# Attention and feed-forward in one kernel: three score steps in any two of three banks, one exponential for both heads in the first pairs, and rests copied by VectorE or GpSimd

## The chip, the cores and the metric

One core of one Trainium2 chip. The engines are TensorE (PE, matmuls; PEld are its weight loads), VectorE (DVE), ScalarE (ACT), GpSimd (POOL) and SyncE (SP, which issues most DMAs). The metric is the time of one execution in microseconds (us) on the device; lower is better. Three runs of the kernel before took 423.41, 424.69 and 424.93 us.

## The reference

Eight batches, 12 heads, 448 rows, 64 columns a head; then a feed-forward over 8 x 448 = 3584 rows of 768 columns and 2048 hidden columns.

```python
def rmsnorm(x, g):
    rms = np.sqrt(np.mean(x * x, axis=-1, keepdims=True) + 1e-06)
    return x / rms * g
q_n, k_n = (rmsnorm(q, g_q), rmsnorm(k, g_k))
scores = scale * np.matmul(q_n, k_n.transpose(0, 1, 3, 2))
attn = softmax(scores)                       # over the last axis
x = np.matmul(attn, v), heads side by side   # [3584, 768]
h = x @ w_in
g = h * np.clip(h + 3.0, 0.0, 6.0) / 6.0
out = g @ w_out
```

(The softmax and the reordering are abbreviated here; the rest is the reference's text.)

## The kernel before, in words

**Pairs.** Two heads are one *pair*; there are 48 pairs, six to a batch. 448 rows are three full tiles of 128 and a *rest* of 64; the rests of the two heads of a pair share one tile. In the first pairs (`PD` = `MB` = 6) Q, K and V are loaded *dense*: a partition holds seven rows of one head, the two heads lie in the two halves of the partitions, and each block of 64x64 is transposed by itself (14 or 16 small transposes a tensor). From pair 6 on they are loaded in the form of 128 partitions by 4 tiles, with a DMA for the main rows and one or two for the rest.

**The steps of a pair.** Squares (`square`, L398, any of GpSimd, ScalarE), their sums (`sums`, VectorE), the inverse root by Ln and Exp (`rstd`, ScalarE), normalizing (`normalize`: L427 dense, L429 else; GpSimd, or VectorE for the pairs of `DN`, here pairs 0 and 1), transposing (`transposes` by TensorE up to pair 11, a transposing DMA from pair 12 on), and the copies `put_q` (scaled by g' = g_q g_k / 8, L465 and L467) and `put_k`. Then four *score steps*: one for the rest tile (i = NT, both heads in one matmul of 128 rows, a bank of 448 columns) and three for the full tiles (two matmuls of 64 rows, one a head, two banks). Each is followed by its exponentials on ScalarE (`expo`, L492; `expo_head`, L497) into `eR` or `eD`, and by `weigh` (L513), eight or five thin matmuls with V that gather the pair's output and its row sums in the bank `av`. `eR` holds the rest's columns twice, so that both heads can be read as 128 columns. When all four are weighed, `divide` (VectorE) makes x, `x_out` (TensorE, later a DMA) transposes it, `put_x` stores it.

**Banks.** PSUM has eight banks: two double ones `sc` (units 0 and 1, for scores), three single ones `ps` (units 2, 3, 4, for the feed-forward and the transposes) and `av`. Up to pair 7 (`PB` = 8) the score steps come one by one, up to pair 23 (`P3` = 24) two full steps together, from pair 24 on three at once: the third takes units 2 and 3 (`THIRD`), so that one bank is left to the feed-forward until their exponentials are done.

**Feed-forward.** `h_mm` (L561) multiplies x with `w_in` in 16 pieces a batch of six matmuls; ScalarE makes `t_sb` (`relu`, L567) and VectorE the gate (`gate`, L572). `y_mm` (L580) multiplies with `w_out`, 16 matmuls for 384 columns; the result is copied out of its bank (`y_copy`, L379, ScalarE or VectorE) and stored. The weights come by GpSimd's DMA queue (`load_w`), `w_in` in five pieces.

**What sets the order.** All instructions are put in order at build time by a planner (`Plan`) that runs a model of the engines. Each operation has a key, the engines that may do it with their costs, and what it depends on. An engine takes the ready operation with the least key; where several engines may do it, the one with the least of time free plus cost times a factor (`PRICE`, and `FIRST` up to 45 us). Feed-forward items come from two lanes, and fill TensorE by a credit (`share`, `DUE`, `FILL`). DMAs are modelled too (`SLOW`, `BEGIN`, `AHEAD`, `LATE`), and the load of a pair is held back by a small memset on GpSimd (`hold`, L796) until the norms of an earlier pair are done. On the chip each engine then goes through its list in this order, and waits at an instruction until its semaphores are there. So any changed cost or factor can move any instruction.

## Time and profile before

| | |
|---|---|
| median of 3 runs | 424.69 us (423.41 to 424.93) |
| the profiled execution's own time | 423.99 us |
| its span | 422.1 us |
| TensorE's granted clock | 1.0 |
| HBM read, written | 45.61 MB, 11.01 MB |

The span runs from the first instruction to the last. Busy time of an engine is the time in which one of its instructions ran; matmuls are pipelined, and a run of them counts as busy throughout. Lines with `<-` name what ended an engine's idle time. A row of a timeline begins with start and length in us; a row of groups ends with busy us, the mean ns of one, and the idle time before them.

### The profile page before, as it was taken

The page shows a single profiled execution, that of the slowest core. Times are in us where ns is not written, and L with a number is a line of the kernel's source. Part 1 is how long each engine was busy: PE and PEld are TensorE (multiplying, and loading weights), DVE is VectorE, ACT ScalarE, POOL GpSimd, SP SyncE. Part 2 cuts the span into 40 slices and gives each one's busy share as a digit, 9 for nine tenths or more (in the row PEclk, how much of TensorE's full clock was granted, in tenths as well). Part 3 has the DMA queues.
Part 4 walks back from the last instruction along what each step waited for, and adds up shares of the span by engine and source line. Part 5 has one row for each costly group of instructions (what it writes and reads, how often), then busy time and mean ns, then how long its engine had stood idle before and what let it go on. Part 6 is the DMA issues. An engine that isn't in the chain of part 4 may idle for free.

```text
span 422.1 us, 9498 instructions
## 1 busy us (share of the span) xinstructions
PE 406.6 (96%) x3692; PEld 237.1 (56%) x3692; DVE 210.6 (50%) x436; ACT 291.7 (69%) x713; POOL 201.3 (48%) x215
## 2 busy tenths in 40 slices
PE   2989999999999999999999999999999999999997
PEld 1565655455555555555555556565556555555565
DVE  7775978455444676457364664546243152042100
ACT  5899986766888988897869977789583243243211
POOL 5998956747676647756575676681000000000000
PEclk9999999999999999999999999999999999999999
DMA  8999899999998959988896968943420301100122
GB/s 253 252 217 235 155 235 176 198 244 176 189 246 208 245 109 201 233 195 202 158 248 168 248 122 198 255 106 77 76 64 13 88 0 39 75 2 37 76 75 76
DMA packets 124561, 65.12 MB, mean 154 GB/s; under 512 B 77412, under 2 KB 121060, under 8 KB 124516
## 3 DMA queue, kind: packets, MB, share of 16 engines
q1 hardware_dynamic: 116144, 57.76, 61.2%
q0 software_dynamic: 8080, 6.29, 10.2%
q8 instruction: 29, 0.48, 0.5%
q10 hardware_dynamic: 292, 0.46, 0.3%
q14 instruction: 16, 0.13, 0.1%
HBM read 45.61 MB, written 11.01 MB: 134 GB/s over the span
## 4 chain that ended last, share of the span: by engine, by line
PE 81%; ACT 5%; DMA 5%; issue 2%; DVE 2%; POOL 2%; SPq 1%; POOLq 0%; DVEq 0%; ACTq 0%
PE ps L580 34%; PE ps L561 29%; PE av L513 9%; PE sc L476 6%; DMA v_st<-in_v_dram 3%; ACT eD L492 3%; DMA qkT<-qkn 2%; PE ps L476 1%; DMA qk_st<-in_q_dram 1%; POOL qkn L429 1%; DVE ssq L406 1%; ACT t_sb L567 1%; PE ps L446 1%; SPq L376 1%; PE sc L561 1%
## 5 line engine op out<-in xcount | busy, mean ns | idle before, releaser
L561 PE MATMUL ps<-xT,w_in_sb 128*128 128x448 bf16 x750 | 165.4, 352 | 1.5 <-ACT eD L497 1.1
L580 PE MATMUL ps<-w_out_sb,gT 128*128 128x384 bf16 (+1 forms) x896 | 162.5, 323 | 0.0
L572 DVE SCALAR_TENSOR_TENSOR gT<-t_sb,ps 128x448 bf16<-128x448 f32 x125 | 76.9, 620 | 110.5 <-ACT t_sb L567 109.6
L492 ACT ACTIVATE eD<-sc 128x768 bf16<-128x768 f32 x240 | 113.3, 567 | 6.0 <-PE sc L476 5.6
L580 PEld LDWEIGHTS <-gT 128*128 128x128 bf16 x912 | 83.8, 98 | 57.2 <-issue 8.8
L561 PEld LDWEIGHTS <-w_in_sb 128*128 128x128 bf16 x768 | 69.8, 98 | 57.6 <-issue 6.1
L429 POOL TENSOR_TENSOR qkn<-qk_st,rstd 128x512 bf16<-128x512 f32 x84 | 85.2, 1043 | 25.0 <-ACT rstd L419 24.7
L403 POOL TENSOR_TENSOR sq<-qk_st 128x1024 f32<-128x1024 f32 (+2 forms) x50 | 81.6, 1642 | 31.8 <-DMA qk_st<-in_q_dram 18.5
L567 ACT ACTIVATE t_sb<-ps 128x448 f32<-128x448 f32 x125 | 69.8, 562 | 31.1 <-PE ps L561 28.5
L513 PEld LDWEIGHTS <-eD 128*128 128x128 bf16 x1152 | 52.4, 98 | 23.2 <-issue 6.3
L406 DVE TENSOR_REDUCE ssq<-sq 128x16 f32<-128x1024 f32 (+2 forms) x50 | 57.7, 1156 | 8.9 <-POOL sq L403 5.9
L379 ACT COPY y_sb<-ps 128x384 f32<-128x384 f32 (+1 forms) x43 | 20.6, 478 | 57.4 <-PE ps L580 57.3
L513 PE MATMUL av<-vaug,eD 128*128 128x65 bf16 x1152 | 58.9, 194 | 0.0
L476 PE MATMUL sc<-qkT 64*128 64x448 bf16 (+1 forms) x288 | 52.8, 358 | 3.2 <-DVE qkT L467 1.1
L379 POOL CAST vaug<-v_st 128x512 bf16<-128x512 f32 x29 | 17.7, 620 | 39.2 <-PE av L513 38.7
L497 ACT ACTIVATE eD<-ps 128x448 bf16<-128x448 f32 (+2 forms) x72 | 25.1, 419 | 15.7 <-PE ps L476 15.7
L492 ACT ACTIVATE eR<-sc 128x448 bf16<-128x448 f32 x96 | 32.9, 412 | 3.1 <-PE sc L476 2.9
L523 DVE RECIPROCAL rden<-av 128x7 f32<-128x7 f32 x48 | 9.7, 202 | 40.4 <-PE av L513 40.2
L476 PEld LDWEIGHTS <-qkT 64*128 64x128 bf16 (+1 forms) x336 | 15.4, 95 | 22.2 <-issue 14.5
L465 ACT ACTIVATE qkT<-qkT,gprime 128x448 bf16<-128x448 bf16 x36 | 24.8, 691 | 1.7 <-DMA qkT<-qkn 1.7
L529 DVE TENSOR_TENSOR xn<-av,rden 128x384 bf16<-128x384 f32 x42 | 23.4, 557 | 1.5
L513 PEld LDWEIGHTS <-eR 128*128 128x128 bf16 x240 | 16.7, 99 | 7.2 <-issue 1.9
(72 smaller groups left out, 177.8 us busy)
## 6 DMA issues: line engine op xcount, KB each, us to landing
qk_st<-in_k_dram SPq DMA_DIRECT2D x21, 384.0 KB, 4.0
qk_st<-in_q_dram SPq DMA_DIRECT2D x21, 384.0 KB, 5.5
v_st<-in_v_dram SPq DMA_DIRECT2D x21, 384.0 KB, 5.9
out_dram<-y_sb SPq DMA_DIRECT2D x20, 384.0 KB, 2.4
w_out_sb<-in_moe_w_out_dram POOLq DMA_DIRECT2D x4, 768.0 KB, 11.1
out_dram<-y_sb SPq DMA_DIRECT2D x15, 192.0 KB, 2.7
w_in_sb<-in_moe_w_in_dram POOLq DMA_DIRECT2D x3, 768.0 KB, 9.5
v_st<-in_v_dram SPq DMA_DIRECT2D x22, 64.0 KB, 5.7
```

The source lines that it names most:

```text
L379: (eng.copy if eng is nc.scalar else eng.tensor_copy)(out=out, in_=in_)
L403: eng.tensor_tensor(out=sq, in0=x, in1=x, op=A_MULT)
L406: nc.vector.tensor_reduce(out=packed(p, ssq_r[:, p % NR, a]), in_=packed(p, sq_r[m % 2][:, a]), axis=mybir.AxisListType.X, op=A_ADD,)
L429: eng.tensor_tensor(out=qkn_r[p % NQ][:, a].rearrange("p t h d -> p h t d"), in0=qk_st[:, a, p % NS], in1=by[:, a].rearrange("p (h t) -> p ...
L476: nc.tensor.matmul(out=(bank(u[h]) if isinstance(u, tuple) else bank(u, h))[:, 0:S], lhsT=qkT[rows, 0, i * P:(i + 1) * P], rhs=qkT[rows, 1 ...
L492: nc.scalar.activation(out=out, in_=in_, func=EXP, bias=0.0, scale=1.0)
L497: nc.scalar.activation(out=e[:, c:c + cols.stop - cols.start], in_=src[:, cols], func=EXP, bias=0.0, scale=1.0)
L513: nc.tensor.matmul(out=av_ps[:, c:c + n], lhsT=e_part(p, i, h, j), rhs=va[:, i].rearrange("p h d -> p (h d)")[:, h * W:h * W + n], start=f ...
L561: nc.tensor.matmul(out=bank(m)[:, 0:S], lhsT=w_in_sb[:, kt, f * P:(f + 1) * P], rhs=xT[:, kt, b % NX, x_slot(b)], start=(kt == 0), stop=(k ...
L567: nc.scalar.activation(out=t[:], in_=bank(m)[:, 0:S], func=RELU, bias=0.5, scale=1.0 / 6.0,)
L572: nc.vector.scalar_tensor_tensor(out=gT[:, f, (b % 2) * S:(b % 2 + 1) * S], in0=t[:], scalar=1.0, in1=bank(m)[:, 0:S], op0=A_MIN, op1=A_MULT,)
L580: nc.tensor.matmul(out=bank(m)[:, 0:n], lhsT=gT[:, f, c0:c0 + P], rhs=w_out_sb[:, f, c:c + n], start=(f == 0), stop=(f == NFT - 1),)
```

## The change

It has these parts.

1. **Three at once.** `THIRD` is now a list of (2, 3), (3, 4), (2, 4), and the planner takes whichever two are free. `P3` goes from 24 to 32, `PB` from 8 to 4. While a burst is due, feed-forward may take banks 3, 2 and 4, not 4 alone.
2. **One early exponential.** In the first six pairs (`TURNED` = 6) the second head's score is made in two matmuls, rest columns first, so that the two heads of a full step lie in one even pattern and one exponential of 896 columns does both. Before there were two: 768 main columns, 128 rest columns.
3. **Rests repeated.** The second copy of `eR`'s rest columns is no longer a second exponential of 64 columns but a copy within `eR` by GpSimd or VectorE (`repeat`), and `weigh` of a rest waits for it.
4. **K and V dense only in pairs 0 and 1** (`PK` = 2); Q stays dense up to pair 5. K and V of pairs 2 to 5 come in the other form; K of these pairs is loaded in the other form, with rest loads and cleared rests of its own, transposed in four pieces instead of 16, and squared with a padded eighth block.
5. **Start.** VectorE normalizes only K of pair 0; the rest goes to GpSimd. Q of pair 1 comes by SP, not by ScalarE's queue. g' is mixed by GpSimd. `w_in` comes in six pieces (256, 256, 256, 256, 512, 512).
6. **The planner's figures**: prices, due times, DMA model, keys, and holds.

What the two built programs hold, by engine (only what differs and matters):

| engine, operation | before | after |
|---|---|---|
| PE transposes 64x64 of Q, K | 168 (+12 of zeros) | 112 (+4) |
| PE transposes 128x128 of Q, K | 48 | 64 |
| PE scores cut into 384 and 64 columns | 0 | 18 |
| ACT exponentials of 64 rest columns into eR | 48 | 0 |
| ACT exponentials 768 and 128 columns | 120 and 120 | 110 and 110 |
| ACT exponentials 896 columns | 0 | 18 |
| ACT exponentials by head (three at once) | 72 | 48 |
| repeat on POOL, on DVE | 0, 0 | 31, 17 |
| casts of V on ACT, on POOL | 19, 29 | 7, 41 |
| copies of y on ACT, on DVE | 44, 13 | 7, 50 |
| memsets on DVE ahead of the first sums | 20 | 23 |

The diff, cut to its core:

```diff
-    PRICE, FIRST, UNTIL = {"POOL": 0.5, "ACT": 1.5, "DVE": 1.5}, {"POOL": 0.5, "ACT": 1.7, "DVE": 1.0}, 45e3
+    PRICE, FIRST, UNTIL = {"POOL": 0.4, "ACT": 2.0, "DVE": 1.5}, {"POOL": 0.6, "ACT": 1.5, "DVE": 0.9}, 45e3
-    SLOW, BEGIN, TIRED = 0.85, 3.6e3, 1.0
+    SLOW, BEGIN, TIRED = 1.1, 3.6e3, 0.95
-    DUE, SOON, FILL = -600, 0, -3000
-    LONG, LEFT = 0.25, 0
+    DUE, SOON, FILL = -900, 300, -3000
+    LONG, LEFT = 0.5, 0
...
-    W_IN = 512, 256, 256, 512, 512
+    W_IN = 256, 256, 256, 256, 512, 512
...
-    DENSE, PD, MB = 2 * NT + 1, 6, 6
+    DENSE, PK, PD = 2 * NT + 1, 2, 6
...
+    def is_dense(a, p):
+        return p < (PK, PD, PK)[a]
...
             nc.tensor.matmul(
-                out=(bank(u[h]) if isinstance(u, tuple) else bank(u, h))[:, 0:S], lhsT=qkT[rows, 0, i * P:(i + 1) * P], rhs=qkT[rows, 1, 0:S],
-                start=True, stop=True,
-            )
+            to = (bank(u[h]) if isinstance(u, tuple) else bank(u, h))[:, 0:S]
+            parts = [(to, slice(0, S))]
+            if i < NT and h and p < TURNED:
+                parts = [(to[:, 0:REST], slice(FULL, S)), (to[:, REST:S], slice(0, FULL))]
+            for out, cols in parts:
+                nc.tensor.matmul(out=out, lhsT=qkT[rows, 0, i * P:(i + 1) * P], rhs=qkT[rows, 1, cols], start=True, stop=True)
...
-            parts = (e[:, 0:S], src[:, 0:S]), (e[:, W4:W4 + REST], src[:, FULL:S])
+            parts = ((e[:, 0:S], src[:, 0:S]),)
...
+            if p < TURNED:
+                out = bass.AP(e.tensor, e.offset, [e.ap[0], [S + REST, 2], [1, S]])
+                nc.scalar.activation(out=out, in_=src[:, :, 0:S], func=EXP, bias=0.0, scale=1.0)
+                return
...
+    def repeat(eng, p):
+        e = eR_t[:, p % NER]
+        eng.tensor_copy(out=e[:, W4:W4 + REST], in_=e[:, FULL:S])
...
-    FF = [(3,), (2,), (4,), (1,), (0,)], [(4,)]
-    THIRD = (2, 3)
+    FF = [(3,), (2,), (4,), (1,), (0,)], [(3,), (2,), (4,)]
+    THIRD = (2, 3), (3, 4), (2, 4)
...
-    W_AFTER, LA, VL = 2, 3, 1.2
-    DN = ((0, 0), (0, 1), (1, 0), (1, 1))
-    MG, EACH = 12, 0.5
-    V0, V2, LATER, AHEAD = 2.5, 0.8, -1, 2500
+    W_AFTER, LA, VL = 2, 4, 1.2
+    DN = ((0, 0),)
+    MG, EACH = 6, 0.5
+    V0, V2, LATER, AHEAD = 2.5, 0.8, -1, 3000
...
-        held[p] = [add((-5, p), [...], norms[p - (5 if p < 12 else LA)] + norms.get(p - NS, []))]
+        held[p] = [add((0, p), [...], norms[p - (4 if p < 18 else LA)] + norms.get(p - NS, []))]
...
-            load(1, 1, 1, 0, 0, nc.scalar, "ACT")
+            load(1, 1, 1, 0, 0, *Q1)
...
-        st = p - 2 if p < HP else p + -1.5
+        st = p - 2 if p < HP else p + 1
...
-            want = [(*THIRD, 0, 1)] if third else [(0, 1)] if len(todo) == 2 else SC if half[0] else RESTS
+            want = [(*t, 0, 1) for t in THIRD] if third else [(0, 1)] if len(todo) == 2 else SC if half[0] else RESTS
...
-                    e = [add((p, 0), [("ACT", 850 if i < NT else 545, lambda p=p, i=i, c=cells[n]: expo(p, i, c["b"]))], [ops[n], old])]
-                    (op.parts[n - 1] if third else op.gives).append(e[0])
+                    e = [add((p, 0), [("ACT", 440 if i == NT else 800 if p < TURNED else 850, lambda p=p, i=i, c=cells[n]: expo(p, i, c["b"]))], [ops[n], old])]
+                    (op.parts[n + 1] if third else op.gives).append(e[0])
+                    if i == NT:
+                        e.append(by((p, 0.5), 160, 100, lambda eng, p=p: repeat(eng, p), e))
...
-            PB, P3 = 8, 24
+            PB, P3 = 4, 32
```

`by` adds an operation that GpSimd or VectorE may do. `Q1` is an empty tuple, so the load goes to SP.

More of the change, by code (lines that the diff above doesn't have):

```diff
@@ L204, in run @@
                     continue
-                if op.calm is not None and (self.backlog("SP", "ACT") > op.calm[0] + 0 or self.backlog("POOL") > op.calm[1]):
+                if op.calm is not None and (self.backlog("SP", "ACT") > op.calm[0] + 1000 or self.backlog("POOL") > op.calm[1]):
                     continue
@@ L834, in stats @@
         else:
-            s2 = [add((st, 3), [("DVE", 1000 if p < PD else 1130, lambda: sums(p, both, m))], s1 + busy)]
+            s2 = [add((st, 3), [("DVE", 1000 if p < PK else 1130, lambda: sums(p, both, m))], s1 + busy + [zero])]
         squares.append(s2[-1])
```

155 lines of the change are left out of this document (82 added, 73 removed).

## The prediction

> **What bounds the kernel now.** The page first: how full TensorE (PE) is, and where its 40 slices are not full.
>
> ```profile
> span 422.1 us, 9498 instructions
> PE 406.6 (96%) x3692; PEld 237.1 (56%) x3692; DVE 210.6 (50%) x436; ACT 291.7 (69%) x713; POOL 201.3 (48%) x215
> PE   2989999999999999999999999999999999999997
> ```
>
> PE is busy 96% of 422.1 us, so nothing can be won by making another engine faster as such: only where PE stands still, or is busy with thin work. The second view gives the busy time of each engine by stage (the columns are PE, PEld, DVE, ACT, POOL with their instruction counts, clock, DMA share, GB/s).
>
> ```profile
> 0.00:40.60 40.60, 30.43 (x468) 19.48 (x469) 28.67 (x77) 33.73 (x92) 33.77 (x53) 1.00 1.06 244
> 40.60:80.00 39.40, 38.56 (x388) 22.75 (x387) 31.68 (x64) 32.23 (x78) 28.55 (x30) 1.00 1.05 182
> 80.00:172.00 92.00, 92.00 (x846) 51.97 (x845) 50.05 (x98) 74.08 (x176) 58.54 (x56) 1.00 1.05 207
> 172.00:186.00 14.00, 12.94 (x124) 7.17 (x123) 7.86 (x17) 12.79 (x33) 9.72 (x10) 1.00 0.91 200
> 186.00:300.00 114.00, 113.81 (x1073) 66.31 (x1072) 62.33 (x125) 92.96 (x238) 70.72 (x68) 1.00 0.79 174
> ```
>
> From 40.6 us on PE is full but for 0.8 us before 80 and 1.1 us around 180. The first 40.6 us are another matter: PE has 468 matmuls there, mostly of 64 and 65 columns. In that stretch there is no feed-forward to fill it, since that needs all six pairs of batch 0. What PE waited for, over the whole span:
>
> ```profile
> PE ps L446 <- DVE qkn L427: 7.1, 2, 6.6
> PE sc L476 <- DVE qkT L467: 1.1, 1, 1.1
> PE ps L561 <- ACT eD L497: 1.1, 2, 0.9
> PE sc L476 <- ACT qkT L465: 0.8, 1, 0.8
> PE ps L561 <- DVE y_sb L379: 0.2, 1, 0.2
> ```
>
> So four places can give time: the start, the 0.8 us of one transposed pair, the 1.1 us behind exponentials, and 0.2 us behind one copy of y on VectorE. What paces the start is the ScalarE queue (start us, us, line, tile, count):
>
> ```profile
> 9.38 0.56 ACT L401 ACTIVATE sq<-qk_st 128x448 f32<-128x448 f32 x1
> 9.97 0.66 ACT L492 ACTIVATE eR<-sc 128x448 bf16<-128x448 f32 x2
> ...
> 15.97 0.66 ACT L492 ACTIVATE eR<-sc 128x448 bf16<-128x448 f32 x2 [0.60 <-PE sc L476]
> ...
> 17.03 1.86 ACT L492 ACTIVATE eD<-sc 128x768 bf16<-128x768 f32 x4
> 18.73 0.26 ACT L417 ACTIVATE lnv<-ssq 128x14 f32<-128x14 f32 x1
> ...
> 35.52 0.67 ACT L492 ACTIVATE eR<-sc 128x448 bf16<-128x448 f32 x2
> 36.09 2.73 ACT L492 ACTIVATE eD<-sc 128x768 bf16<-128x768 f32 x6
> ```
>
> The rest exponential (eR) opens each pair: pair 0 at 9.97, pair 1 at 15.97, pair 6 at 35.52. Pairs 1 to 5 take 19.55 us back to back; pair 0 takes 6.0, because PE's scores of pair 1 come late. The bulk of the feed-forward begins here, 5.1 us after pair 5's exponentials:
>
> ```profile
> 40.65 1.49 PE L561 MATMUL ps<-xT,w_in_sb 128*128 128x448 bf16 x7
> ```
>
> **The change, part by part.** PE's total work stays: 64 fewer 64x64 transposes, 16 more of 128x128, 18 scores cut in two, two fewer score bursts. All but the bursts lie in the first six pairs, beside ScalarE's queue, and count nothing there. If that cover went, the transposes would save and the cuts cost under 1 us each.
>
> *Exponentials.* A full step (two heads, main and rest exponential) takes (18.73 - 17.03)/2 = 0.85 us of ScalarE. One of 896 columns I work out from these rows:
>
> ```profile
> L492 ACT ACTIVATE eD<-sc 128x768 bf16<-128x768 f32 x120 | 99.5, 830 | 6.0 <-PE sc L476 5.6
> L492 ACT ACTIVATE eR<-sc 128x448 bf16<-128x448 f32 x48 | 27.3, 570 | 3.1 <-PE sc L476 2.9
> L492 ACT ACTIVATE eR<-sc 128x64 bf16<-128x64 f32 x48 | 12.2, 254 | 0.0
> L379 ACT CAST vaug<-v_st 128x512 bf16<-128x512 f32 x19 | 11.9, 633 | 2.0 <-PE av L513 2.0
> L379 ACT COPY y_sb<-ps 128x384 f32<-128x384 f32 x41 | 19.9, 486 | 55.6 <-PE ps L580 55.5
> L379 DVE COPY y_sb<-ps 128x384 f32<-128x384 f32 x13 | 7.2, 557 | 16.1 <-PE ps L580 15.7 <-issue 0.3
> ```
>
> (830 - 570)/320 = 0.81 ns a column, so 896 columns end after 934 ns; the two ended after 1.01 us (1.86 - 0.85). I take 0.06 us less a step, and 0.1 less a rest (0.66 against 0.57). Over pairs 1 to 5: 15 x 0.06 + 5 x 0.1 = 1.4 us less. But the changed order puts more on the same stretch of ScalarE: three casts of V (0.52 each by their spacing) where there were none, six squares instead of three (0.52 each), against one put_q and one pair of rstd fewer (0.56 and 0.39). Net: 19.55 - 1.4 + 1.56 + 1.56 - 0.95 = 20.3 us. So **the early exponential does not shorten the pairs**; it only pays for the other moves.
>
> *The start.* Four rows of before, then the new order.
>
> ```profile
> 2.14 0.47 SPq L359 DMA_DIRECT2D qk_st<-in_q_dram  x1
> 4.71 1.31 DVE L406 TENSOR_REDUCE ssq<-sq 128x7 f32<-128x448 f32 x2 [0.40 <-ACT sq L401]
> 9.07 1.82 POOL L403 TENSOR_TENSOR sq<-qk_st 128x448 f32<-128x448 f32 x2 [2.04 <-DVE ssq L406]
> 12.37 0.94 POOL L427 TENSOR_TENSOR qkn<-qk_st,rstd 128x448 bf16<-128x448 f32 x1
> ```
>
> VectorE has a few small memsets more ahead of its first sums (4.71 becomes about 5.1). Only K of pair 0 is normalized by VectorE; Q of pair 0 goes to GpSimd (0.94 instead of 0.62) and pair 1 too, behind two squares of pair 2 and 3. With 0.9 to 1.0 us an instruction GpSimd is then at: Q0 to 7.8, squares to 10.0, norms of pair 1 to 11.8, cast of V to 12.4, K2 to 13.4. Pair 0's first exponential stands behind the square of Q2 as before. The load of Q2 goes out sixth instead of fourth on SP, behind three waits of the queue, about 3 us later than its 2.14, but behind the same bytes: I leave 9.97, with +1.0 as the other end. In PE's order pair 1's rest score comes behind the transposes of K2 (13.4), so it is done at about 14.6 and ScalarE, whose own work up to there is 4.6 us (a rest, three steps, a square, a cast and two rstd), begins pair 1 at **14.7 instead of 15.97**. Then pair 6 opens at 14.7 + 20.3 = 35.0. After pair 5's exponentials the new order has only one weigh (0.25), the division (0.2 + 0.62), x_out (0.3), its copy (0.39) and four hops of about 0.1 ahead of the bulk: 37.2, not 40.65. PE has then left undone one rest score, four full scores, one weigh and one matmul of the feed-forward: 0.19 + 4 x 0.24 + 0.25 + 0.19 = 1.6 us. Gain: 3.4 - 1.6 = **1.8 us**. Bounds: +1.0 (late Q2, GpSimd in the way), -3.0 (the whole idle ScalarE time of pair 0 and its tail).
>
> *The wait for pair 12* (0.8 us): PE came to its score before the transposing DMA and ScalarE's scaling were through.
>
> ```profile
> 78.91 0.35 PE L476 MATMUL sc<-qkT 128*128 128x448 bf16 x1 [0.82 <-ACT qkT L465]
> ```
>
> In the two orders PE has 126 h and 5 y matmuls ahead of it before, 133 and 32 after: 5 us more work. The wait goes: **-0.8**, +0.8 if the loads come as much later (rest loads held by other norms).
>
> *Three steps at once.* Their four banks may now be any two of the feed-forward's, and they begin at pair 32, not 24. The wait in the 180s:
>
> ```profile
> 184.07 0.62 ACT L379 CAST vaug<-v_st 128x512 bf16<-128x512 f32 x1
> 184.58 1.04 ACT L497 ACTIVATE eD<-ps 128x448 bf16<-128x448 f32 x3
> ...
> 185.18 2.05 PE L561 MATMUL ps<-xT,w_in_sb 128*128 128x448 bf16 x10 [0.85 <-ACT eD L497]
> ```
>
> A cast of V on ScalarE stood ahead of the exponentials that free the banks. Casts there fall from 19 to 7, and 41 copies of y to 7 (48 x 0.1 of rest exponentials go too): I take **-1.0** of the 1.1, bounds -1.5 and 0. What is late next is VectorE.
>
> *Copies of y.* 50 instead of 13 on VectorE. 13 made one wait of 0.2; 37 more make 0.2 x 37/13 = **+0.5** (0 to +1.0: some will stand behind a sum of 1.2 us).
>
> *Repeats.* 31 on GpSimd, 17 on VectorE; no row shows one. The nearest are the small ones (254 ns for 64 columns on ScalarE, 620 for a 512-column cast on GpSimd): I take 0.2 us, off the path, for a rest's weigh starts 1 to 2 us behind its score. Behind a repeat wait PE's queue and so everything; that is a rival below.
>
> Sum: -1.8 - 0.8 - 1.0 + 0.5 = -3.1. The profiled run took 423.99 us (422.1 of span, 1.9 around it), 0.7 below the median of 424.69 and within its runs. 423.99 - 3.1 = **420.9 us**.
>
> **Rivals.**
>
> *Given back (423.7).* The 1.8 us rest on GpSimd keeping time at the start. It is busy 33.77 of the first 40.6 us; if it or the load of Q2 eats the gain (0), half of the three-step wait stays (-0.5) and VectorE's copies cost the whole 1.0, what is left with pair 12's 0.8 is -0.3. For it: the terms that no row shows all point this way. Against: GpSimd's norms of pairs 3 to 5 come 3 us or more ahead of their need.
>
> *GpSimd's repeats hold PE (427).* PE's queue waits at 31 weighs for a copy on GpSimd, which stands in order behind squares that wait for loads:
>
> ```profile
> POOL vaug L379 <- PE av L513: 38.7, 13, 6.3
> POOL sq L403 <- DMA qk_st<-in_q_dram: 18.5, 7, 4.9
> ```
>
> In the new order 14 of the 31 have such a square within four instructions ahead. If half of the 18.5 us falls on them, less PE's lead of 1.2 us at each of 3.5 places, 5 us reach PE, and a third of the gains goes too: 420.9 + 5 + 1 = 427. It decides as soon as a load is over 1.2 us later than GpSimd comes to it. Against: casts of V have the same place on GpSimd in 29 cases, PE needs them too, and it waited for none; GpSimd itself waited 38.7 us for PE there. A stall this long would also cool TensorE by the Trainium skill ("TensorE: Matmul & The Clock Gate", Part 1: the clock is halved after an idle window of about 3.4 us); no wait of PE here is that long once it runs, so no row shows it, and it would add to the 427.
>
> *A repeat on VectorE waits out GpSimd (423.4).* 17 repeats read and write SBUF on VectorE while GpSimd is busy 58.54 of 92 us with instructions of 1 to 1.9 us. If a repeat can't run beside one, it waits 0.6 x 0.9 us on average, 10 us of VectorE in all; a quarter of it (VectorE is half busy) reaching PE through late gates is +2.5. The rule is in the Trainium skill ("SBUF — State Buffer", "SBUF: two separate sides"): the two engines share a port pair that one instruction holds alone, for VectorE's fast two-port copies. Before has no such copy on VectorE, so the trace neither bears it out nor excludes it.
>
> *All at the good ends (418.7).* -3.0 at the start, -0.8, -1.5, no cost of the copies: -5.3. For it: ScalarE, at 74 of 92 us the busiest beside PE, sheds 34 copies and 12 casts. Against: PE's listed waits after 40 us come to little over 2 us.
>
> **How the numbers follow.** Forecast 0.42 (419.3 to 422.8), given back 0.25, GpSimd's repeats 0.17, VectorE's 0.07, more 0.09. About 0.5% (2.1 us) is what a measurement of this kernel can tell from no change: below 422.6 is faster, above 426.8 slower. Faster: 0.38 of the forecast's 0.42, and 0.09: 0.47. Same: 0.04 + 0.25 + 0.06 = 0.35. Slower: 0.17 + 0.01 = 0.18. The range goes from 417.5 to 426.0: it holds the forecast, "given back", "more" and VectorE's, and leaves out most of the 427.
>
> **What would show it.** Right: pair 1's rest exponential at 14.7 and the bulk of h at 37.2; no wait of PE for ScalarE's qkT near 80; waits of L561 for eD under 0.3 in sum. Wrong: a row of PE av waiting for GpSimd's or VectorE's eR of over 1 us in sum; many rows of PE waiting for y_sb; the bulk of h after 39.

## The result, and the profile after

The changed kernel takes 423.0 us (median of 10 runs, 421.34 to 425.17) against 424.56 us of the kernel before beside it: a ratio of 0.9962, with a 95% interval from 0.9944 to 0.9979. That is a gain, but of 1.6 us where 3.1 were forecast (420.9). It lies in the stated range (417.5 to 426.0), but above the part that the prediction called its forecast (419.3 to 422.8), and above 422.6, its border for a gain that a measurement can tell. The profiled run took 422.97 us (420.9 of span), 1.0 us less than the profiled run of before.

The page of the changed kernel: PE is as full as it was, and the hole is again in the first slices.

```profile
span 420.9 us, 9447 instructions
PE 405.0 (96%) x3662; PEld 234.4 (56%) x3662; DVE 238.2 (57%) x489; ACT 262.0 (62%) x584; POOL 216.8 (52%) x260
PE   2888999999999999999999999999999999999997
```

The same five stages as before (the columns are PE, PEld, DVE, ACT, POOL, clock, DMA share, GB/s):

```profile
0.00:40.60 40.60, 28.21 (x428) 18.71 (x429) 29.25 (x80) 31.79 (x63) 32.70 (x52) 1.00 1.04 220
40.60:80.00 39.40, 39.28 (x402) 23.07 (x401) 29.72 (x64) 28.67 (x65) 30.99 (x37) 1.00 1.18 231
80.00:172.00 92.00, 92.00 (x830) 50.54 (x828) 54.96 (x106) 69.83 (x157) 61.76 (x71) 1.00 0.88 187
172.00:186.00 14.00, 14.00 (x134) 8.02 (x133) 8.85 (x17) 11.29 (x26) 12.25 (x12) 1.00 0.86 204
186.00:300.00 114.00, 113.80 (x1053) 65.08 (x1051) 68.86 (x135) 86.87 (x208) 77.27 (x87) 1.00 0.88 182
```

Two stages carry the gain. From 40.6 to 80 us PE is busy for 39.28 us instead of 38.56, and from 172 to 186 for 14.00 instead of 12.94: 0.72 + 1.06 = 1.8 us of standing still are gone. What PE still waits for (its first matmul of g, at 5.7 us, left out):

```profile
PE ps L559 <- DVE xn L541: 2.2, 4, 0.8
PE sc L485 <- ACT eR L502: 1.5, 1, 1.5
PE sc L485 <- ACT eD L496: 0.6, 2, 0.4
PE ps L450 <- DVE qkn L431: 0.6, 1, 0.6
```

All of these lie before 40 us; behind it PE waits twice for 0.2 us, for VectorE. No row names a transposed pair scaled by ScalarE, y_sb, or a repeat as what PE's av waits for. The start is the other half of the result. ScalarE's queue there, and the first stretch of the feed-forward's bulk on PE:

```profile
10.46 0.58 ACT L406 ACTIVATE sq<-qk_st 128x448 f32<-128x448 f32 x1 [1.57 <-DMA qk_st<-in_q_dram]
10.94 0.53 ACT L502 ACTIVATE eR<-sc 128x448 bf16<-128x448 f32 x1
...
16.40 0.54 ACT L502 ACTIVATE eR<-sc 128x448 bf16<-128x448 f32 x1 [0.83 <-PE sc L485]
17.34 0.92 ACT L496 ACTIVATE eD<-sc 128x896 bf16<-128x896 f32 x1 [0.40 <-PE sc L485]
...
35.39 1.73 ACT L496 ACTIVATE eD<-sc 128x896 bf16<-128x896 f32 x2 [0.59 <-PE sc L485]
...
38.32 0.54 ACT L502 ACTIVATE eR<-sc 128x448 bf16<-128x448 f32 x1 [0.16 <-PE sc L485]
...
39.84 1.49 PE L576 MATMUL ps<-xT,w_in_sb 128*128 128x448 bf16 x7
```

Pair 0 opens at 10.94 (before 9.97), pair 1 at 16.40 (15.97; forecast 14.7), pair 6 at 38.32 (35.52; forecast 35.0), and the bulk begins at 39.84 (40.65; forecast 37.2). By the prediction's own arithmetic, 1.6 us of PE's work are then undone that were done before: the start **lost** 1.6 - 0.8 = 0.8 us instead of winning 1.8. (The traces agree: from the begin of the bulk to the end PE is busy for 377.5 us, 376.1 before.) With the 1.8 us of the two stages that gives -1.0, near the 1.2 us by which the span is shorter.

One group is far from what was assumed (mean in ns of one):

```profile
L507 DVE COPY eR<-eR 128x64 bf16<-128x64 bf16 x17 | 9.2, 541 | 4.2 <-ACT eR L502 4.2
L507 POOL COPY eR<-eR 128x64 bf16<-128x64 bf16 x31 | 7.3, 234 | 35.3 <-ACT eR L502 35.2
```

The same copy of 64 columns takes 234 ns on GpSimd, but 541 on VectorE.

### The profile page after: what moved, and what is told of

Same layout as the page of the kernel before. It is cut to its first block, busy times and chain, and to the rows that moved or that the text cites. A ratio compares the mean times of both kernels' runs of the same rounds, so it can differ in the third digit from the quotient of the medians.

```text
span 420.9 us, 9447 instructions
## 1 busy us (share of the span) xinstructions
PE 405.0 (96%) x3662; PEld 234.4 (56%) x3662; DVE 238.2 (57%) x489; ACT 262.0 (62%) x584; POOL 216.8 (52%) x260
## 4 chain that ended last, share of the span: by engine, by line
PE 90%; ACT 3%; DVE 2%; DMA 2%; SPq 1%; issue 1%; POOL 0%; ACTq 0%; POOLq 0%
PE ps L595 35%; PE ps L576 33%; PE av L528 11%; PE sc L485 8%; DMA v_st<-in_v_dram 1%; PE ps L485 1%; ACT eD L496 1%; DMA qk_st<-in_q_dram 1%; PE ps L457 1%; ACT eD L502 1%; DVE xn L541 1%; PE sc L576 1%; DVE eR L507 0%; ACT eR L502 0%; PE ps L559 0%
## 5 line engine op out<-in xcount | busy, mean ns | idle before, releaser
L595 PE MATMUL ps<-w_out_sb,gT 128*128 128x384 bf16 (+1 forms) x912 | 167.9, 323 | 0.0
L502 ACT ACTIVATE eD<-sc 128x768 bf16<-128x768 f32 x220 | 103.5, 561 | 18.3 <-PE sc L485 14.9
L433 POOL TENSOR_TENSOR qkn<-qk_st,rstd 128x512 bf16<-128x512 f32 x88 | 89.8, 1039 | 26.4 <-ACT rstd L423 26.3
L412 DVE TENSOR_REDUCE ssq<-sq 128x16 f32<-128x1024 f32 (+1 forms) x50 | 58.0, 1166 | 12.8 <-POOL sq L408 9.6
L383 DVE COPY y_sb<-ps 128x384 f32<-128x384 f32 (+1 forms) x50 | 27.5, 549 | 66.2 <-PE ps L595 65.4
L485 PE MATMUL sc<-qkT 64*128 64x448 bf16 (+3 forms) x322 | 54.5, 350 | 3.0 <-ACT eR L502 1.5
L383 POOL CAST vaug<-v_st 128x512 bf16<-128x512 f32 x41 | 25.1, 615 | 29.9 <-PE av L528 29.1
L502 ACT ACTIVATE eR<-sc 128x448 bf16<-128x448 f32 x48 | 26.6, 554 | 7.9 <-PE sc L485 6.7
L512 ACT ACTIVATE eD<-ps 128x448 bf16<-128x448 f32 (+2 forms) x48 | 16.7, 420 | 17.8 <-PE ps L485 17.8
L507 POOL COPY eR<-eR 128x64 bf16<-128x64 bf16 x31 | 7.3, 234 | 35.3 <-ACT eR L502 35.2
```

The source lines that it names most:

```text
L383: (eng.copy if eng is nc.scalar else eng.tensor_copy)(out=out, in_=in_)
L412: nc.vector.tensor_reduce(out=ssq_r[:, p % NR, a, 0:nb], in_=sq_r[m % 2][:, a, 0:nb], axis=mybir.AxisListType.X, op=A_ADD)
L433: eng.tensor_tensor(out=qkn_r[p % NQ][:, a].rearrange("p t h d -> p h t d"), in0=qk_st[:, a, p % NS], in1=by[:, a].rearrange("p (h t) -> p ...
L485: nc.tensor.matmul(out=out, lhsT=qkT[rows, 0, i * P:(i + 1) * P], rhs=qkT[rows, 1, cols], start=True, stop=True)
L502: nc.scalar.activation(out=out, in_=in_, func=EXP, bias=0.0, scale=1.0)
L595: nc.tensor.matmul(out=bank(m)[:, 0:n], lhsT=gT[:, f, c0:c0 + P], rhs=w_out_sb[:, f, c:c + n], start=(f == 0), stop=(f == NFT - 1),)
```

## The experiments

Most kernels here keep the order of every engine as the changed kernel has it and alter only what one step issues ("order unchanged"). Where the planner had to plan anew, that is said. The kernels were measured in four groups (e1 to e4, e5 to e8, e9 to e12, e13 to e16), each beside runs of its own of the kernel before. So between groups the ratios are the safer measure; 0.001 of a ratio is 0.4 us.

**e1: Q of pairs 2 and 3 loaded first.** The three loads swap their places in SP's queue:

```
 K2-5 rest lo, K2-5 rest hi, Q2-3 main   ->   Q2-3 main, K2-5 rest lo, K2-5 rest hi
```

> The order of every engine but SP stays; the load of Q of pairs 2 and 3 is issued ahead of the two loads of K's rests of pairs 2 to 5, which come behind it. Theory 'late load' (the start lost time because ScalarE stood 1.57 us at the square of Q2): pair 0's first rest exponential at about 9.7 instead of 10.94, pair 1's at about 15.2 instead of 16.40, and the whole 0.8 to 1.2 us sooner, about 422.0. Rival 'two loads, one of them late': K2's rests now land some 1.5 us later, GpSimd's squares of K2 and K3 stand ahead of pair 1's norms, so the first exponential is at 9.7 all the same, but pair 1's at 16.4 to 17.4, and the time is 423.0 to 424.0.

Measured: 424.96 us, ratio to before 1.0017 (0.9991 to 1.0044), 2 us worse than the changed kernel.

```profile
9.53 0.54 ACT L502 ACTIVATE eR<-sc 128x448 bf16<-128x448 f32 x1
16.64 0.54 ACT L502 ACTIVATE eR<-sc 128x448 bf16<-128x448 f32 x1 [0.84 <-PE sc L485]
```

Pair 0 opens 1.4 us sooner, pair 1 no sooner: the rival holds, the rests are as much needed as Q. But the loss of 2 us is more than it foretold; e2 shows what else was at work.

**e2: the early exponential undone**, order unchanged:

```
-            if i < NT and h and p < TURNED:      (score cut in two)
+            if i < NT and h and p < 0:
-            if p < TURNED:                       (one exponential of 896)
+            if p < 0:
```

> The early exponential undone alone, in an unchanged order: the first six pairs' full steps are again a score per head and two exponentials (768 and 128 columns). The part-by-part theory: ScalarE paces pairs 1 to 5, each step costs 0.2 us more by the rows (818 + 293 against 914), so pair 6's rest exponential goes from 38.3 to 40.8 to 41.3 and the time to 425 to 426. Rival 'something else paces the pairs by now' (VectorE with its sums of 1.2 us, GpSimd with its norms): pair 6 opens before 39.3, and the time stays under 424.

Measured: 424.83 us, ratio 1.0002 (0.9977 to 1.0027). The time is near the first theory, yet pair 6 opens at 39.63, not at 41, although the clock of this run dips ahead of it (0.50 from 22 to 25 us; e3 says more of such dips). The stretch in which the time was lost, VectorE's repeat of pair 1 and GpSimd's queue beside it:

```profile
15.71 1.05 POOL L433 TENSOR_TENSOR qkn<-qk_st,rstd 128x512 bf16<-128x512 f32 x1
...
16.41 3.72 DVE L507 COPY eR<-eR 128x64 bf16<-128x64 bf16 x1
16.72 0.93 POOL L431 TENSOR_TENSOR qkn<-qk_st,rstd 128x448 bf16<-128x448 f32 x1
17.60 0.61 POOL L383 CAST vaug<-v_st 128x512 bf16<-128x512 f32 x1
18.17 1.92 POOL L408 TENSOR_TENSOR sq<-qk_st 128x448 f32<-128x448 f32 x2
```

The copy of 64 columns began while GpSimd was at work and ended at 20.13, 0.04 us after the last of five instructions that GpSimd ran without a pause. PE waited for it:

```profile
PE av L528 <- DVE eR L507: 2.5, 1, 2.5
```

In e1 the same repeat took 2.97 us, and PE waited 1.8 for it. In the profiled run of the changed kernel it was let in after a single norm (0.25 us). So e1 and e2 are both disturbed by a thing they were not meant to test, and are made again below without it (e8, e7).

**e3: the rest columns made twice by ScalarE**, as before; no repeat at all; order unchanged:

```
-            parts = ((e[:, 0:S], src[:, 0:S]),)
+            parts = (e[:, 0:S], src[:, 0:S]), (e[:, W4:W4 + REST], src[:, FULL:S])
-                        e.append(by((p, 0.5), 160, 100, lambda eng, p=p: repeat(eng, p), e))
+                        e.append(by((p, 0.5), 160, 100, lambda eng, p=p: None, e))
```

> The repeats undone alone, in an unchanged order: ScalarE makes the second copy of the 64 rest columns from PSUM by a second exponential, as before, and VectorE and GpSimd repeat nothing. If the repeats are free and ScalarE paces the start: pair 6 opens 5 x 0.25 = 1.2 us later (39.6), the later 42 cost nothing much, and the time is about 424.0. Rival 'repeats cost' (541 ns each on VectorE, behind GpSimd): the time falls to 422 or below although pair 6 opens later.

Measured: 422.28 us, ratio 0.9950 (0.9930 to 0.9971), 0.7 us better than with the repeats, though the intervals overlap. ScalarE's 48 additional exponentials cost nothing that shows, and the repeats perhaps did. Its profiled run shows a second thing. Here are two stretches of it by stage:

```profile
32.00:34.50 2.50, 1.13 (x20) 0.69 (x19) 1.72 (x3) 2.41 (x6) 0.26 (x2) 1.00 1.20 250
34.50:38.00 3.50, 3.50 (x32) 2.27 (x33) 0.39 (x1) 2.65 (x6) 3.50 (x5) 0.51 1.52 189
```

After 2.5 us in which PE was busy for 1.13, its granted clock (third column from the right) is 0.51 for 3.5 us. At that rate PE does 1.7 us less. The profiled run of the changed kernel is nearly as thin in the same 2.5 us (1.32) and keeps its clock: the thin stretch does not bring a dip each time. The kernel before is not thin there:

```profile
32.00:34.50 2.50, 2.34 (x38) 1.50 (x38) 1.04 (x4) 2.50 (x7) 2.50 (x4) 1.00 1.20 257
```

Such a dip shows in a run's mean clock as 0.996 or less. Of the 139 runs of the changed kernel and the experiments on it (e11 left out) 56 have one; of the 42 runs of e9 and e14 to e16, which have the start of before, none has. The kernel before itself, in its 131 runs beside the experiments, has 7. In e6, runs with a dip have a median of 423.14 and runs without one of 421.54: 1.6 us; in the other kernels the difference lies between 0.6 (e12) and 3.5 us (e5).

**e4: the free choice of banks undone**, planned anew from about half of the program on:

```
-    FF = [(3,), (2,), (4,), (1,), (0,)], [(3,), (2,), (4,)]
-    THIRD = (2, 3), (3, 4), (2, 4)
+    FF = [(3,), (2,), (4,), (1,), (0,)], [(4,)]
+    THIRD = (2, 3),
```

> The free choice of banks undone alone (planned anew from about half of the program on; the start stays): three steps at once only in the two banks that they had before, the feed-forward keeps to the third while they are due. Theory 'the banks won the late part' (2.3 us between 45 us and the end): 424.3 to 425.5, with a wait of PE for eD of over 1 us in sum. Rival 'fewer casts and copies on ScalarE won it, or the other order': 423.0 within 0.5.

Measured: 425.96 us, ratio 1.0044 (1.0019 to 1.0068): 3 us more than the changed kernel, and slower than before. Where they are lost, e4 first, then the changed kernel:

```profile
172.00:186.00 14.00, 14.00 (x131) 7.80 (x131) 8.85 (x18) 10.86 (x25) 12.25 (x13) 1.00 0.91 210
225.00:270.00 45.00, 43.65 (x413) 25.11 (x413) 26.08 (x50) 33.61 (x83) 35.63 (x39) 1.00 1.01 200
270.00:315.00 45.00, 43.92 (x407) 25.12 (x404) 21.43 (x49) 32.38 (x78) 16.78 (x24) 1.00 0.40 98
```

```profile
225.00:270.00 45.00, 44.80 (x448) 26.60 (x446) 27.08 (x54) 30.86 (x75) 28.09 (x32) 1.00 0.87 174
270.00:315.00 45.00, 45.00 (x410) 25.97 (x407) 25.38 (x54) 35.48 (x86) 23.92 (x27) 1.00 0.56 121
```

PE stands still for 1.35 + 1.08 = 2.4 us where the changed kernel stands still for 0.2, from just behind where three steps at once begin (215 us in both). ScalarE has its casts and copies taken off here too (7 and 11 are left): that relief alone does not do it. But from 172 to 186 us, where the kernel before stood still, PE is full here as well, with fixed banks: no three steps run at once there yet. In the kernel before they begin at 166.8 us.

**e5: the repeat in steps of two**, order unchanged:

```
-        eng.tensor_copy(out=e[:, W4:W4 + REST], in_=e[:, FULL:S])
+        out, in_ = (x.rearrange("p (c t) -> p t c", t=2) for x in (e[:, W4:W4 + REST], e[:, FULL:S]))
+        eng.tensor_copy(out=out, in_=in_)
```

> The repeats stay where they are, and the same 64 columns are copied, but in two interleaved passes (every second column), so that neither side runs through memory in steps of one. Theory 'port': VectorE's fast copy between SBUF tiles can't run beside an instruction of GpSimd and waits until one ends (in the traces so far it ends 0.04 us after one, and took up to 3.72 us); the slow form needs no fast mode, so the mean on VectorE falls from 541 ns to under 250, the longest under 0.45 us, no PE wait names eR on VectorE, and the time is 421.5 to 422.5. Rival 'any VectorE access to SBUF waits there': mean over 450 ns as before, 423.0. GpSimd's own repeats get no shorter in either.

Measured: 423.44 us, ratio 0.9985 (0.9959 to 1.0012). The theory falls, as far as it spoke of a fast mode that steps of one need:

```profile
L508 DVE COPY eR<-eR 128x64 bf16<-128x64 bf16 x17 | 11.0, 648 | 4.2 <-ACT eR L502 4.2
```

The copy still waits (648 ns). It is not the steps of one that make it wait. In which mode VectorE made these copies, the run doesn't tell.

**e6: all repeats on GpSimd**, order unchanged:

```
-                        e.append(by((p, 0.5), 160, 100, lambda eng, p=p: repeat(eng, p), e))
+                        e.append(by((p, 0.5), 160, 100, lambda eng, p=p: repeat(G, p), e))
```

> All 48 repeats on GpSimd, in an unchanged order. The prediction's rival 'GpSimd's repeats hold PE': the 17 that move stand behind squares and norms of 1.0 us (and behind waits for loads), PE av waits for eR on GpSimd for over 2 us in sum, and the time is 424.5 to 427. Theory 'port': GpSimd's copy of 234 ns costs GpSimd 17 x 0.23 = 4 us in all, which the idle 200 us hide; PE waits under 0.5 us, and the time is 421.5 to 422.8.

Measured: 422.17 us, ratio 0.9934 (0.9908 to 0.9959).

```profile
L507 POOL COPY eR<-eR 128x64 bf16<-128x64 bf16 x48 | 11.3, 235 | 36.2 <-ACT eR L502 36.1
```

All 48 take 235 ns, no wait of PE names one, and pair 6 opens at 37.48 instead of 38.32. The prediction's rival, that GpSimd's repeats hold PE, is refuted even with 48 of them (in e10, which has them too, one wait of 0.5 us names one).

**e7: the early exponential undone, without repeats** (the edits of e2 and e3 together), order unchanged.

> e2 again without the repeats: ScalarE makes the rest columns twice (as in e3) and the early steps are two exponentials again, order unchanged. To be compared with e3 (422.28), which has no copy that could wait. If ScalarE paces pairs 1 to 5: 15 x 0.2 = 3 us more, pair 6 at 41 to 42.7 and the time at 424.3 to 425.3. If something else paces them: pair 6 within 1 us of e3's 39.7, the time under 423.

Measured: 424.08 us, ratio 0.9982 (0.9964 to 1.0000), 1.8 us more than e3 (1.4 by the ratios). In this order the early exponential is worth 1 to 2 us; the prediction gave its 15 steps 0.9. Where pair 6 opens can't be compared: the clock dips ahead of it in both profiled runs.

**e8: Q first, without repeats** (the edits of e1 and e3 together), order unchanged.

> e1 again without the repeats: rest columns made twice on ScalarE (as in e3) and Q of pairs 2 and 3 loaded ahead of K's rests. To be compared with e3 (422.28). 'Late load': the first rest exponential 1.2 us sooner and all behind it, 421.1 to 421.6. 'Two loads, one of them late': the first at 9.6, pair 1's at 16.3 or later, 422.3 to 423.0.

Measured: 423.60 us, ratio 0.9972 (0.9947 to 0.9996), 1.3 us more than e3 (0.9 by the ratios, and the intervals overlap). Pair 0 opens at 9.53 and pair 1 at 16.60, where e3 has 10.96 and 16.26. One of the two loads is late, whichever goes first.

**e9: part 1 alone, on the kernel before**: the two lines of e4 the other way round, and the lines that carry the chosen banks to the scores and exponentials; planned anew from pair 24 on.

> The kernel before with part 1 alone: three steps at once take any two of the feed-forward's three banks (still from pair 24 on), planned anew from there; the start is that of before. If the free banks won the late part: the prediction's -1.0 (bounds -1.5 and 0) of 424.6 gives 423.6, and PE's wait for eD of 1.1 us is gone. If they won the 2.3 us that the changed kernel gains behind its start: 422.3. Rival 'the relief of ScalarE won it': 424.6 as it was, with the wait for eD still over 0.8 us.

Measured: 424.04 us, ratio 0.9976 (0.9950 to 1.0001): 1.0 us less, as much as the prediction gave it, but the interval reaches no change, and the medians (424.41 before) are only 0.4 apart. The trace says more. Two stages of its profiled run:

```profile
40.60:80.00 39.40, 38.71 (x389) 22.81 (x387) 31.30 (x64) 32.14 (x78) 28.42 (x31) 1.00 1.05 185
...
172.00:186.00 14.00, 14.00 (x125) 8.05 (x124) 6.64 (x12) 12.40 (x33) 9.94 (x12) 1.00 1.08 238
```

The wait of the 180s is gone with ScalarE about as loaded as before (36 copies of y and 18 casts are left on it), though three steps at once begin at 164.5 us here; the wait of pair 12 is still there.

**e10: no hole in the stream of loads**, on e6; order else unchanged:

```
-            lg = plan.dma((1, 1.2), 2, 40, lambda: load_g(nc.scalar), queue="ACT")
+            lg = plan.dma((1, 1.2), 2, 40, lambda: load_g(nc.gpsimd), queue="ACT")
 (and the two memsets of xn on VectorE, behind pair 0's put_q, instead of GpSimd)
```

The rows of the changed kernel that it undoes: SP's two loads of K's rests take 2.24 us to issue, and Q goes out only at 4.89.

```profile
2.61 2.24 SPq L380 DMA_DIRECT2D qk_st<-in_k_dram  x2
4.89 0.60 SPq L363 DMA_DIRECT2D qk_st<-in_q_dram  x1
```

> e6 (all repeats on GpSimd) with the two loads of g on GpSimd's queue instead of ScalarE's, so that they take none of the eight places in flight and SP need not wait 1.4 us at K's second rest load; GpSimd's two memsets of xn go to VectorE, which is idle there; else the order is e6's. Theory 'hole in the stream of loads': Q of pairs 2 and 3 lands at about 9.3 instead of 10.4 and K's rests at 7.4, pair 0's first rest exponential opens at 9.9 (e6: 11.16), pair 1's at 15.2 (16.07), pair 6's at 36.6 (37.48), and the time is 421.2 (e6: 422.17). Rival 'the transfers bound it': Q still lands after 10 and nothing moves, 422.2.

Measured: 422.36 us, ratio 0.9933 (0.9906 to 0.9961), as e6.

```profile
9.62 0.58 ACT L406 ACTIVATE sq<-qk_st 128x448 f32<-128x448 f32 x1 [0.32 <-DMA qk_st<-in_q_dram]
...
15.29 0.54 ACT L502 ACTIVATE eR<-sc 128x448 bf16<-128x448 f32 x1 [0.55 <-PE sc L485]
...
37.06 0.54 ACT L502 ACTIVATE eR<-sc 128x448 bf16<-128x448 f32 x1 [0.33 <-PE sc L485]
```

Q's square begins 0.8 us sooner than in the changed kernel, pair 1 opens 0.8 us sooner than in e6, pair 6 still 0.4, and the time does not move. The late load was real, and is not what holds the time.

**e11: more work for PE in the start**, on e6:

```
-                nc.tensor.transpose(...)
+                for _ in range(3 if p < 8 else 1):
+                    nc.tensor.transpose(...)
```

> e6 with the 128x128 transposes of pairs 2 to 7 done three times over instead of once (the same result into the same place): 48 more matmuls of 56 ns, 2.7 us of PE work in the first 40 us and no other change. Theory 'clock': the granted clock halves for 3.4 us where PE has been thin for some microseconds (it did in 4 of e6's 9 runs, at 1.6 us each); with more work it halves in fewer than 1 of 10, and the median is e6's of undisturbed runs plus up to 0.5: 421.5 to 422.0. Rival 'more work is more work': the halving stays as frequent, and the time is 422.2 plus up to 1.5.

Measured: 424.02 us, ratio 0.9975 (0.9948 to 1.0003). The clock dips in 1 of 12 runs instead of 4 of 9, which fits the theory of the clock, in few runs. But the filler, 64 matmuls and 3.6 us of work (the expectation's count of 48 was too low), costs more than the dips: 1.9 us against e6.

```profile
39.43 0.54 ACT L503 ACTIVATE eR<-sc 128x448 bf16<-128x448 f32 x1 [1.06 <-PE sc L486]
```

Up to pair 6 PE is busy for 28.20 us instead of e6's 25.28. Pair 6 opens 1.95 us later, and ScalarE waited for PE's score. So thin work of PE is not free in the start.

**e12: K and V of pairs 2 to 5 dense**, as before, on e6; planned anew:

```
-    DENSE, PK, PD = 2 * NT + 1, 2, 6
+    DENSE, PK, PD = 2 * NT + 1, 6, 6
```

> e6 with K and V of pairs 2 to 5 in the dense layout of before (one load without rests, 14 transposes of 64x64 for each K instead of 4 of 128x128), planned anew. Theory 'K's layout cost the start': no rest loads stand ahead of Q of pairs 2 and 3, so Q lands at about 9.0 and the first rest exponential opens at 9.8; GpSimd's squares and norms get 0.1 us shorter each; PE's extra thin work of 1.7 us lies beside ScalarE and keeps the clock up (no run with a clock under 0.998); pair 6 opens at 36 to 37 and the time is 420.8 to 421.8. Rival 'the layout is a gain': PE's extra transposes reach pair 6, which opens after 38, and the time is over 422.5.

Measured: 425.48 us, ratio 1.0006 (0.9977 to 1.0035), 3.3 us more than e6, although pair 6 opens at 36.44, 1 us sooner: a part of each theory. PE now waits for GpSimd's norms instead:

```profile
PE ps L450 <- POOL qkn L431: 2.5, 6, 0.8
```

The opening of pair 6 alone is no measure of the start; what PE has left undone by then belongs to it. Since all of the order is another, this says little on the layout by itself.

**e13: casts of V of pairs 1, 3 and 5 on GpSimd**, on e6, order unchanged:

```
-                               ("ACT", 530, lambda p=p: cast_v(A_, p))],
+                               ("ACT", 530, lambda p=p: cast_v(G if p < HP else A_, p))],
```

> e6 with the casts of V of pairs 1, 3 and 5 on GpSimd instead of ScalarE, at the same places of the order. Theory 'ScalarE's new work paces the start' (the prediction counted three casts and three squares more on it, 3.1 us): pairs 1 to 5 shrink from 21.4 us (e6) to 19.8, pair 6 opens at about 36.0 and the time falls to 421.0. Rival 'the chain through PE and GpSimd paces it': 1.9 us more on GpSimd, which is busy 19 of the 22 us there, push norms and squares back, pair 6 opens at 37.5 to 39, time 422.2 to 423.2.

Measured: 423.26 us, ratio 0.9948 (0.9922 to 0.9974), 1.1 us more than e6 (0.6 by the ratios, and the intervals overlap). Taking 1.9 us off ScalarE wins nothing when GpSimd gets them. Pair 5 opens at 34.53, in e6 at 33.27:

```profile
34.53 0.53 ACT L502 ACTIVATE eR<-sc 128x448 bf16<-128x448 f32 x1
```

Pair 6 (40.16) can't be compared: the clock of e13's profiled run dips just ahead of it.

**e14: the start of before with the late parts**, planned anew: e9 with

```
-            PB, P3 = 8, 24
+            PB, P3 = 8, 32
+                    if i == NT and p >= 6:
+                        e.append(add((p, 0.5), [("POOL", 160, lambda p=p: repeat(G, p))], e))
 (and one rest exponential from pair 6 on)
```

> The start of before (dense K, norms on VectorE, loads and early exponentials as they were) with the late parts: free banks, three steps from pair 32 on, one rest exponential from pair 6 on with the repeat on GpSimd; planned anew. If the start of the changed kernel gives nothing: PE work undone at 45 us as in before (365.0 us at full rate), stalls behind that fall from 8.8 to 6.5 us, and the time is 422.0, with no run whose clock falls. If the late gain needs the y copies on VectorE or the new start as well: stalls behind 45 us of 7.8 as in e9, 423.6 to 424.

Measured: 421.86 us, ratio 0.9917 (0.9886 to 0.9949): the lowest ratio of all, 3.2 us under the 425.01 of before beside it, with no dip of the clock in its 6 runs. The interval overlaps with those of e6, e10 and e3.

**e15: e14 with the early exponential** of pairs 0 to 5.

> e14 and the early exponential (heads 1 turned, one exponential of 896 columns in pairs 0 to 5), with no other change of the start or the order. The prediction's 15 x 0.06 and e7's measured 1.8 us are two sizes of it: 0.9 to 1.8 us off pairs 1 to 5, pair 6 at 34.3, the time 420.5 to 421.3. Rival 'in this order something else paces the pairs' (PE's thin transposes): pair 6 within 0.4 us of e14's, the time equal.

Measured: 422.77 us, ratio 0.9935 (0.9911 to 0.9958). Where pair 6 opens in e15, then in e14:

```profile
35.52 0.54 ACT L498 ACTIVATE eR<-sc 128x448 bf16<-128x448 f32 x1
```

```profile
35.35 0.55 ACT L492 ACTIVATE eR<-sc 128x448 bf16<-128x448 f32 x1
```

In the order of before the early exponential brings nothing that shows: the rival holds.

**e16: e14 with y copied on VectorE nearly always** (48 of its 55 wide copies, instead of 14), planned anew:

```
-    PRICE = {"POOL": 0.5, "ACT": 1.5, "DVE": 1.5}
+    PRICE = {"POOL": 0.4, "ACT": 2.0, "DVE": 1.5}
```

> e14 with the planner's late prices of the changed kernel, by which y is copied on VectorE nearly always instead of mostly on ScalarE. If the relief of ScalarE by these copies makes part of the late gain: stalls behind 45 us 0.5 to 1.0 us less than e14's, the time 421.0 to 421.5. By the prediction's term of +0.5 (37 more copies behind sums): 0.5 more than e14.

Measured: 423.67 us, ratio 0.9966 (0.9940 to 0.9993), 1.8 us more than e14, with intervals that just touch. Its profiled run is one of its short ones (422.33) and shows no wait for y_sb, so which wait makes the longer ones (up to 426.06) stays open.

## Why the prediction was wrong, step by step

**The start (forecast -1.8, came out at +0.8): the step that failed.** The step was "begins pair 1 at 14.7 instead of 15.97. Then pair 6 opens at 14.7 + 20.3 = 35.0", and the bulk at 37.2. The bulk began at 39.84, 2.6 us later: 1.7 up to pair 1, 1.6 in pairs 1 to 5 (21.9 us instead of 20.3), less 0.7 by a shorter tail. The step failed because it let ScalarE's queue alone set the pace and held all else to be beside it:

- *Up to pair 1.* The load of Q took the +1.0 that had been named as its other end, but ScalarE then stood 0.83 us ahead of pair 1 all the same. Pair 1's score stands in PE's list behind the transposes of K2, and these waited for GpSimd, which stood for two loads itself, K's rests and V:

```profile
8.65 2.04 POOL L408 TENSOR_TENSOR sq<-qk_st 128x512 f32<-128x512 f32 x2 [0.87 <-DMA qk_st<-in_k_dram]
...
13.28 0.62 POOL L383 CAST vaug<-v_st 128x512 bf16<-128x512 f32 x1 [0.80 <-DMA v_st<-in_v_dram]
13.85 1.04 POOL L433 TENSOR_TENSOR qkn<-qk_st,rstd 128x512 bf16<-128x512 f32 x1
```

K2 is normalized at 14.89, where the prediction's list for GpSimd had 13.4: 1.5 of the 1.7 us. In e10, with the loads sooner, it is 13.77, pair 1 opens 1.1 us sooner, and the time of the whole stays. So this is not all that decided, and e1 and e8 show that another order of loads only makes the rests late.
- *Pairs 1 to 5.* ScalarE's own work was added up rightly: it is busy for 20.41 of the 21.92 us, where the forecast had 20.3 for the whole. What the sum left out is that ScalarE stands still for the other 1.5 us (0.3 of 19.55 before), most of it waiting for PE's scores (0.40, 0.59 and 0.16 in the rows above; about the same in e10, with neither a late load nor a VectorE repeat).
- *A wait that no term had.* Ahead of the 0.59 it looks like this:

```profile
33.88 0.62 DVE L541 TENSOR_TENSOR xn<-av,rden 128x448 bf16<-128x448 f32 x1
34.56 0.34 PE L559 MATMUL ps<-identity,xn 128*128 128x128 bf16 x3 [0.77 <-DVE xn L541]
34.98 0.56 PE L485 MATMUL sc<-qkT 64*128 64x448 bf16 x6
```

PE's list has the transposing of the last pair's x (`x_out`, L559) ahead of the next full scores, and PE stands until VectorE has divided (L541): so ScalarE waits for VectorE by way of PE. This is the first row of PE's waits above, four times, 2.2 us in all. Every profiled run with the new start has it, with 0.8 to 2.6 us; those with the start of before have 0.3 or none. No run takes it away alone, so what it costs is not shown.
- *"Count nothing there", of PE's thin work.* e11 refutes it: some 3 us more of it put pair 6 back by 1.95. The change itself made this work less (PE is busy for 28.21 instead of 30.43 us up to 40.6), so it is not what the start lost. A second exponential on ScalarE costs 1.4 to 1.8 us (e7 against e3), and 1.9 us moved from ScalarE to GpSimd win nothing (e13). In the start the engines pace each other, and work moved from one to the next is not hidden. The change moved three casts and three squares onto ScalarE and three norms onto GpSimd; the early exponential paid for a part of that. In the order of before, without these moves, it brings nothing that shows (e15), and e14, with that start and the late parts, is no slower than any kernel with the new one.
- *The repeats on VectorE*, and the *dips of the clock*, which the step did not have at all: see below.

**The wait of pair 12 (-0.8): right.** 0.72 us by stage, and the row is gone. e9, which has the free banks but not the other order, keeps it (0.69 us), so it was not the banks.

**Three steps at once (-1.0): right in size, in part in its cause.** 1.06 us by stage. The prediction named three things: the banks, the later begin, and the cast that no longer stood ahead of the exponentials. In the changed kernel the later begin is enough for the wait of the 180s: three steps run at once only from 215 us on, and e4, with fixed banks, is as full from 172 to 186. The free banks are enough as well: e9 has them, begins at 164.5, has the casts and copies on ScalarE, and the wait is gone. What they are worth in the changed kernel shows behind 225 us: without them, e4 loses 2.4 us, although its casts and copies are taken off. Taking the cast off was not needed.

**Copies of y on VectorE (+0.5): nothing in the trace** of the changed kernel. e16, whose late part is planned anew, hints at up to 1.8 us, by a way that no profile shows. Added up, the profiled run has +0.8 - 0.7 - 1.1 = -1.0 where -3.1 was forecast: the +0.5 that did not come hides a part of the miss in the start.

**Repeats ("0.2 us each off the path"): right for GpSimd (234 ns), wrong for VectorE (541).** The rival "a repeat on VectorE waits out GpSimd" had the mechanism, and at 423.4 nearly the time, but a chance of 0.07. By it, the repeats beside GpSimd wait 0.5 us on average; shown are 0.3 us more than on GpSimd on average, and 1.8 and 2.5 us of PE when one in the start is not let in for long (e1, e2). Moving them to GpSimd is worth 0.8 us at pair 6 and about as much in the median (e6), though the intervals overlap. In the changed kernel most are let in after one instruction of GpSimd, even where the next follows without a pause. This one ended at 35.52, behind the first of three norms of 1.0 us:

```profile
34.45 3.04 POOL L433 TENSOR_TENSOR qkn<-qk_st,rstd 128x512 bf16<-128x512 f32 x3 [2.32 <-ACT rstd L423]
34.83 0.69 DVE L507 COPY eR<-eR 128x64 bf16<-128x64 bf16 x1 [0.33 <-ACT eR L502]
```

Why the one of e2 waited for five instructions, no run shows. The trace agrees with the Trainium skill ("SBUF — State Buffer", "SBUF: two separate sides") in that one of the two engines is blocked for the other's whole instruction. That section of the Trainium skill ties it to VectorE's fast two-port copies and to operations with two inputs in SBUF; the repeat has one input, and no run here shows the mode in which VectorE made it.

**Of the rivals**, "given back" (423.7) has the start right, whose gain went, but not the later terms, which did not shrink; VectorE's 423.4 is nearest as a number, by a cost of 2.5 us that the changed kernel's trace does not show. "GpSimd's repeats hold PE" is refuted by e6. The clock was named beside that rival as a rule of the Trainium skill ("TensorE: Matmul & The Clock Gate", Part 1: a halved clock after an idle window of some 3.4 us) with the remark that no wait of PE is that long. In e3 no wait in the 2.5 us ahead of the dip is longer than 0.8 us, and the clock fell: a thin stretch can be enough, and the measurement decides. For the changed kernel's median this is small (2 of its 10 runs dip), for e6 more.

Of the prediction's own signs, those of being right came for the late terms (no wait for qkT near 80 us, none of h for eD), and one of being wrong for the start: the bulk of h after 39.

**What stays open:** how much of the 0.8 us lost in the start the late loads, PE's wait for x, the repeats and GpSimd's norms each have by themselves, since a single profiled run of the same start opens pair 6 anywhere from 37.46 (e4) to 38.32; and what the y copies on VectorE do in e16.

## What to carry to other kernels

Where no engine is full and the pace is set by a chain that goes round several engines, price a move on each engine of the round: there is no "beside". Count the whole gain only from a late, comparable place, with the work that is undone there, not from the opening of one step. And before a small SBUF-to-SBUF copy goes to VectorE, look at what GpSimd does beside it: the copy may wait until an instruction of GpSimd ends, and at times until several have.

## What the runs showed of the hardware that was not expected

- Of the 17 copies of 128x64 bf16 from SBUF to SBUF on VectorE in the profiled run of the changed kernel, 16 ended 0.04 to 0.06 us after an instruction of GpSimd did. They took 541 ns on average, against 234 ns for the same copy on GpSimd. Most waited for one instruction; one in e2 waited over five (3.72 us), and one in e1 took 2.97 us. In steps of two the copy waits as much (648 ns).
- The granted clock of TensorE fell to 0.51 for 3.5 us after 2.5 us in which PE was busy for 1.13, with no wait over 0.8 us (e3); with 1.32 in the same stretch it did not (the changed kernel's profiled run). Dips came in 56 of 139 runs of the changed kernel and the experiments on it, in none of 42 runs of e9 and e14 to e16, and in 7 of 131 of the kernel before, which is busy for 2.34 of the same 2.5 us. In e6 a run with one takes 1.6 us more.
